# An attention stage whose steps all get new positions, and the row-sum reciprocals of the stage behind it set closer together

## The chip, the cores and the metric

The kernel runs on one core of a Trainium2 chip. The metric is device time in microseconds (us), the median of several executions. TensorE is called PE below, VectorE DVE, ScalarE ACT, GpSimd POOL, and SyncE, which here only issues transfers, SP. Each engine runs its own instructions strictly in the order in which they stand in the program.

## The reference

```python
q_pool = q.reshape(B, H, S // 2, 2, D).mean(axis=3)          # B, H, S, D = 8, 8, 1152, 64
scores = np.matmul(q_pool, k.transpose(0, 1, 3, 2)) / np.sqrt(D)
scores = scores - np.max(scores, axis=-1, keepdims=True)
attn = np.exp(scores)
attn = attn / (np.sum(attn, axis=-1, keepdims=True) + 1e-09)
x = merge_heads(np.matmul(attn, v))                          # [8, 576, 512]
theta = x @ w_theta
y = einsum('ts,bsd->btd', w_tok_r, x * cos(theta)) + einsum('ts,bsd->btd', w_tok_i, x * sin(theta))
u = x + y
out = u + np.maximum(u @ w_ch, 0.0)
```

Everything is float32. The kernel keeps that precision by splitting an operand into a rounded high part and the remainder (hi and lo), and adding up three products.

## The kernel before

**Part 1, attention.** The work is cut into 32 pairs of heads, numbered i. A pair passes through these steps, named as in the table `PLACE`:

- SP: `load_q`, `load_k`, `load_v`; `load_max` brings the transposed row maxima (tile nt, L818) back as rows nmrs (L829, L833).
- DVE: `pool_q` (L713) adds neighbouring rows of Q. POOL: `diff` (L720) prepares K. DVE turns the tiles: `t1` (L747, 960 columns) and `t0` (L745, 768 columns), into a PSUM bank each. ACT rounds them, `hi1`, `hi0` (L774), DVE takes the remainders, `lo1`, `lo0` (L778).
- PE and DVE: 15 passes for the row maxima. `pm` (L791) makes one block of scores from the high parts alone, `mx` (L803) reduces it. After `mx22`, the last, come `nm` (L815) and `nt` (L818).
- PE, ACT, POOL: 18 blocks of exact scores, `e` (L851), whose exponentials are taken by `x` (L861, tile pc) with the maxima that ACT's `rn` (L836, tile nmrr) has rounded. POOL adds them up, `ss` (L868). PE multiplies with V, `av` (L873), and sums over partitions, `ns` (L894).
- The reciprocals of the sums: `norm_recip` (L920). For the first eight pairs they are multiplied in here (`norm_out`, L944; `norm_turn`, L949), for the others in part 2.

The maxima of pair i+2 run beside the scores of pair i+1 and the products with V of pair i, so one period of this pipeline is one pair. Beside it, 18 small jobs prepare the weights (`w_max` L1027, `w_shift` L1031, `w_sign` L1038, `w_mask` L1044 on DVE; `w_mul`, `w_add` on POOL; ten `w_turn` on PE). They are "side" steps.

The order is made on the host before the program is built. `operations` lists every step with its engine, and `schedule` sorts each engine's steps by `PLACE[step] + 18 * i`, for the weights by `w0 + wd * job + wk * step`; it decides when side steps are put in, and it may look a few steps ahead at the start and the end. A score tile of PSUM is a bank: `t`, `pm`, `e`, `av` and `ns` share four pairs of them, and a step that takes a bank waits until its last reader is done. So a `pm` that takes over the bank of `t1` waits for `lo1`.

**Part 2, token and channel mixing.** Eight batches b follow each other, each step put at a number `at2(...)` (56 to a batch). For b > 1, the reciprocals for each quarter c of x are loaded by `dnload` (L1190) into the tile dn, of which there is one, and multiplied in by `dnmul` (L1194); then `xblock` (L1218, L1219) stores x turned, POOL makes the remainder xl (L605), and PE computes the angles pth (L1237). PE works on batch b-1 meanwhile: py (L1325), pr (L1364), the step `relu` (L1377), which DVE does and which frees PE's bank, and the output stores (`oblock`, L1385 and L1388). `dnload` and `dnmul` stand at:

```python
at2(base + DN_AT[0] + 0.1 + DN_AT[1] * c, dnload, b, c)
at2(base + DN_AT[0] + DN_AT[2] + DN_AT[1] * c, dnmul, b, c)
```

Of the kernel before, what the change touches and what calls it, by code (L numbers as in the profile page):

```python
# [22 lines left out]
NU = 18  # L23
CHAINS = ((0, 0, 0), (0, 1, 0), (0, 0, 1), (0, 1, 1), (0, 0, 2), (0, 1, 2), (0, 2, 0), (1, 0, 0), (0, 2, 1), (1, 0, 1), (0, 2, 2), (1, 0, 2), (1, 1, 0), (1, 2, 0), (1, 1, 1), (1, 2, 1), (1, 1, 2), (1, 2, 2))
PLACE = {
# [40 lines left out]
}  # L66
LOOK = 8
LATE = 2.0
# [11 lines left out]
THETA_AT = (-42.4, -33.8, -25.1, -15.4, -9.2)  # L80
XHI0_AT = 568.5
XB_AT = -55.0
DN_AT = (-79.5, 6.8, 6.4)
TH0_BANK = "hmmrh"
XN_AT = -4.0
XN0_BANK = "tmmrt"
# [422 lines left out]
def pooled_attention_moe_kernel(  # L509
# [638 lines left out]
    with ExitStack() as p2:  # L1148
# [17 lines left out]
        def at2(pos, fn, *args):  # L1166
            todo2.append((pos, len(todo2), fn, args))
# [251 lines left out]
        for b in range(B):  # L1419
            base = CYC * b  # L1420
            if b > 0:
                at2(base + DN_AT[0] if b > 1 else X1_AT, xload, b)
                if b > 1 and b % 2 == 0:
                    at2(base + DN_AT[0] + 0.2, dwload, b)
                    at2(base + DN_AT[0] + DN_AT[2] + 0.1, dwmul, b)
                for c in range(ND if b > 1 else 0):
                    at2(base + DN_AT[0] + 0.1 + DN_AT[1] * c, dnload, b, c)
                    at2(base + DN_AT[0] + DN_AT[2] + DN_AT[1] * c, dnmul, b, c)
            if b == 0:
# [75 lines left out]
```

## Time and profile before

| | us |
|---|---|
| median of 3 runs | 1281.33 (1281.25 to 1281.88) |
| profiled execution | 1282.72 |
| span in its trace | 1280.9 |
| PE busy | 1223.0 (95%) |
| DVE busy | 959.9 (75%) |
| POOL busy | 809.3 (63%) |
| ACT busy | 676.9 (53%) |

The numbers below are from the profiled execution, which is 1.39 us above the median; 1.8 us of it lie outside the span. The granted clock is 0.998 of full speed. Part 1 takes about 800 us of the span. The average busy share says little here: PE is nearly always busy, so a step's place matters only where PE stops for it.

### The profile page before, as it was taken

What the parts mean: (1) busy time and instruction counts of PE and PEld (TensorE: products, weight loads), DVE (VectorE), ACT (ScalarE), POOL (GpSimd) and SP (SyncE); (2) the same over time, 40 slices, a digit from 0 to 9 for tenths busy, and PEclk for the clock granted to TensorE, in tenths of its full rate; (3) what the DMA queues carried; (4) which work ended last, traced back from release to release, by engine and by line L of the source; (5) the groups of instructions that cost most, each with busy time, mean ns of one, the idle gap of its engine ahead of it and who ended that gap; (6) DMA issues with size and microseconds to landing.
All of it is one profiled execution on the core that took longest, in us unless ns stands there. A gap on an engine that the chain in (4) does not pass through costs nothing.

```text
span 1280.9 us, 27779 instructions
## 1 busy us (share of the span) xinstructions
PE 1223.0 (95%) x10915; PEld 952.1 (74%) x10915; DVE 959.9 (75%) x1313; ACT 676.9 (53%) x1129; POOL 809.3 (63%) x596
## 2 busy tenths in 40 slices
PE   4899999999999999999999999999999999999998
PEld 2566666666766666666666666698999999989998
DVE  6788898998788888878887887255675757657553
ACT  1456656656666665666565666464343443344331
POOL 1588988898887898788888788533423233242320
PEclk9999999999999999999999999999999999999999
DMA  7435555557455454545545541216654646455332
GB/s 119 83 77 134 110 96 123 127 115 158 85 101 93 104 120 85 113 92 100 117 90 104 90 98 39 62 57 150 127 102 105 134 109 135 95 120 116 85 55 37
DMA packets 489403, 130.16 MB, mean 102 GB/s; under 512 B 459576, under 2 KB 460280, under 8 KB 489272
## 3 DMA queue, kind: packets, MB, share of 16 engines
q1 hardware_dynamic: 489272, 128.39, 48.8%
q8 instruction: 85, 1.39, 0.5%
q14 instruction: 46, 0.38, 0.1%
HBM read 97.61 MB, written 29.52 MB: 99 GB/s over the span
## 4 chain that ended last, share of the span: by engine, by line
PE 67%; DVE 11%; ACT 8%; DMA 5%; issue 3%; SPq 3%; POOL 3%; ACTq 0%; DVEq 0%; POOLq 0%
PE b L851 17%; PE b L873 16%; PE py L1325 12%; PE b L791 6%; PE pr L1364 6%; PE pth L1237 5%; ACT pc L861 5%; PE b L894 4%; DVE mx L803 3%; DMA dn<-rod 2%; DMA qn<-in_q_dram 1%; POOL xl L605 1%; POOL ss L868 1%; DMA qk<-in_k_dram 1%; DVE wf L1038 1%
## 5 line engine op out<-in xcount | busy, mean ns | idle before, releaser
L803 DVE TENSOR_REDUCE mx<-b 128x2 f32<-128x768 f32 x480 | 440.4, 951 | 94.8 <-PE b L791 93.7
L868 POOL TENSOR_TENSOR ss<-ss,pc 128x576 f32<-128x576 f32 x314 | 460.9, 1480 | 14.4 <-ACT pc L861 2.0
L861 ACT ACTIVATE pc<-b 128x576 f32<-128x576 f32 x576 | 353.7, 652 | 128.8 <-PE b L851 112.7
L873 PE MATMUL b<-pc,vn 128*64 128x288 f32 x2304 | 306.8, 411 | 0.0
L873 PEld LDWEIGHTS b<-pc,vn 128*64 128x64 f32 x2304 | 154.4, 136 | 111.5 <-issue 21.8
L1325 PE MATMUL py<-wtk,Z 128*128 128x288 f32 x1728 | 234.2, 296 | 0.5 <-DVE uT L1377 0.5
L1325 PEld LDWEIGHTS py<-wtk,Z 128*128 128x128 f32 x1728 | 232.3, 189 | 2.0 <-DVE uT L1377 0.9
L1298 POOL TENSOR_TENSOR Z<-ab,Z 128x512 fp32r<-128x512 f32 x40 | 53.8, 1346 | 266.2 <-ACT Z L1294 266.2
L791 PE MATMUL b<-hi 64*128 64x384 f32 x960 | 180.0, 393 | 24.0 <-DVE mx L803 16.6
L851 PE MATMUL b<-hi 64*128 64x288 f32 x1152 | 191.4, 328 | 11.1 <-ACT pc L861 3.4
L851 PE MATMUL b<-lo,hi 64*128 64x288 f32 x1152 | 171.3, 293 | 0.0
L851 PE MATMUL b<-hi,lo 64*128 64x288 f32 x1152 | 170.8, 292 | 0.0
L791 PEld LDWEIGHTS b<-hi 64*128 64x128 f32 x960 | 90.2, 189 | 93.8 <-DVE mx L803 45.4
L851 PEld LDWEIGHTS b<-hi 64*128 64x128 f32 x1152 | 108.8, 185 | 52.6 <-ACT pc L861 41.4
L868 POOL TENSOR_TENSOR ss<-pc,pc 128x576 f32<-128x576 f32 x64 | 92.1, 1440 | 71.8 <-ACT pc L861 71.7
L851 PEld LDWEIGHTS b<-lo,hi 64*128 64x128 f32 x1152 | 109.8, 187 | 0.0
L851 PEld LDWEIGHTS b<-hi,lo 64*128 64x128 f32 x1152 | 109.5, 186 | 0.0
L1364 PEld LDWEIGHTS pr<-us,wch 128*128 128x128 f32 x768 | 104.1, 188 | 1.5
L1364 PE MATMUL pr<-us,wch 128*128 128x288 f32 x768 | 105.1, 295 | 0.0
L720 POOL TENSOR_TENSOR qk<-qk 128x384 f32<-128x384 f32 x62 | 64.4, 1038 | 64.2 <-DMA qk<-in_k_dram 54.2
L774 ACT CAST hi<-b 128x960 fp32r<-128x960 f32 x64 | 56.3, 881 | 63.2 <-DVE b L747 58.3
L778 DVE TENSOR_TENSOR lo<-b,hi 128x960 fp32r<-128x960 f32 x64 | 66.6, 1053 | 15.1 <-ACT hi L774 13.2
(100 smaller groups left out, 1326.1 us busy)
## 6 DMA issues: line engine op xcount, KB each, us to landing
vn<-in_v_dram SPq DMA_DIRECT2D x32, 576.0 KB
qn<-in_q_dram SPq DMA_DIRECT2D x124, 144.0 KB
qk<-in_k_dram SPq DMA_DIRECT2D x124, 144.0 KB
xd<-xu SPq DMA_DIRECT2D x32, 288.0 KB
xT<-xd SPq DMA_DIRECT2D x8, 1152.0 KB
xn<-xbd SPq DMA_DIRECT2D x140, 64.0 KB
out_dram<-ub SPq DMA_DIRECT2D x124, 72.0 KB
xbd<-xb SPq DMA_DIRECT2D x28, 288.0 KB
```

Of the source, the lines that this page charges most:

```text
L720: (nc.vector if op.eng == DVE else nc.gpsimd).tensor_tensor(kn[:, c : c + W], kn[:, c : c + W], kn[:, c - W : c], ALU.subtract)
L774: nc.scalar.copy(hi, src)
L778: nc.vector.tensor_tensor(lo, src, hi.bitcast(F32), ALU.subtract)
L791: nc.tensor.matmul(pm[:, h, 0:W], hi[hs, q : q + P], hi[hs, group(g)], start=(g == 0), stop=True, skip_group_check=(g > 0),)
L803: nc.vector.tensor_reduce(maxima(op.i)[:, at, g : g + 1], slots[op.slot][:, :, 0:W], AX.X, ALU.max)
L851: nc.tensor.matmul(pe[:, h, 0:HALF], w[hs], x[hs], start=bool(op.acq and n == 0), stop=(n == len(terms) - 1), skip_group_check=not op.acq,)
L861: nc.scalar.activation(pc, slots[op.slot][:, :, 0:HALF], AF.Exp, scale=SC)
L868: nc.gpsimd.tensor_tensor(st["ss", u], first, st["pc"][u, k], ALU.add)
L873: nc.tensor.matmul(half(op)[hs, 0:HALF], st["vn"][:, h, key(u, k), :], st["pc"][u, k][:, h, :], start=(k == 0), stop=(k == KT - 1),)
L1237: nc.tensor.matmul(th, xs[c][:, j * P : (j + 1) * P], ws[:, c], start=(n == 0), stop=(n == 11))
L1325: nc.tensor.matmul(st["py", c, u][:, 0:HALF], Z[zi][:, c * P : (c + 1) * P], wtk[wi][:, kw, u * HALF : (u + 1) * HALF], start=(i == 0 and ...
L1364: nc.tensor.matmul(pr[u][:, 0:HALF], wch[wi][:, c, e * P : (e + 1) * P], st["us", ui][:, c, u * HALF : (u + 1) * HALF], start=(n == 0), st ...
```

## The change

All numbers in `PLACE` are new, so the steps of part 1 stand in another order on every engine, and two of the three numbers of `DN_AT` are smaller. No step is added or taken away, and no other line differs. Of the table two lines stand for all:

```diff
-    "hi10": -21.08587, "lo10": -23.99859, "t00": -24.04688, "hi00": -19.4519, "lo00": -23.47768,
+    "hi10": -21.37568, "lo10": -31.19797, "t00": -30.74071, "hi00": -21.12643, "lo00": -29.5554,
...
-    "ns50": -3.42739, "slack": 0.08481, "turn": 18.16883, "w0": 1.55551, "wd": 33.42062,
-    "wk": 1.74585, "lk": 1, "early00": 8.02425, "xhi00": 525.23001, "xlo00": 492.64828,
+    "ns50": 213.87592, "slack": 0.14937, "turn": 0.45204, "w0": 16.49569, "wd": 33.25011,
+    "wk": 0.28685, "lk": 1, "early00": -61.74543, "xhi00": 523.75714, "xlo00": 622.34897,
...
-DN_AT = (-79.5, 6.8, 6.4)
+DN_AT = (-79.5, 6.2, 6.0)
```

**Place A, DVE in part 1, between nt and the first maxima of the next pair.** Before, in pair 12, which carries a weight job (b1 and b2, b0 and b3 are banks; hi12 and lo12 belong to pair 12):

```order
L818 STREAM_TRANSPOSE nt_135<-nm_133 128x32
L747 STREAM_TRANSPOSE b3_110<-qk12_3446 128x2x480
L745 STREAM_TRANSPOSE b0_107<-qk12_3446 128x2x384
L778 TENSOR_TENSOR lo12_3749<-b3_110,hi12_3748 128x960
L778 TENSOR_TENSOR lo12_3749<-b0_107,hi12_3748 128x768
L803 TENSOR_REDUCE mx12_3782<-b3_110 128x2
L1027 TENSOR_SCALAR ws_3787<-wf_3714 128x576
L1031 TENSOR_SCALAR wf_3714<-ws_3787 128x3x192
L803 TENSOR_REDUCE mx12_3782<-b0_107 128x2
L1038 SCALAR_TENSOR_TENSOR wf_3714<-raw_3552,wf_3714 128x3x192
L803 TENSOR_REDUCE mx12_3782<-b3_110 128x2
```

And of the changed kernel, the same place:

```order
L818 STREAM_TRANSPOSE nt_135<-nm_133 128x32
L747 STREAM_TRANSPOSE b1_108<-qk12_3451 128x2x480
L1027 TENSOR_SCALAR ws_3748<-wf_3701 128x576
L778 TENSOR_TENSOR lo12_3751<-b1_108,hi12_3750 128x960
L745 STREAM_TRANSPOSE b2_109<-qk12_3451 128x2x384
L1031 TENSOR_SCALAR wf_3701<-ws_3748 128x3x192
L778 TENSOR_TENSOR lo12_3751<-b2_109,hi12_3750 128x768
L1038 SCALAR_TENSOR_TENSOR wf_3701<-raw_3545,wf_3701 128x3x192
L803 TENSOR_REDUCE mx12_3804<-b1_108 128x2
L803 TENSOR_REDUCE mx12_3804<-b2_109 128x2
L803 TENSOR_REDUCE mx12_3804<-b1_108 128x2
```

The turn `t0` now stands behind `lo1`, so t and lo alternate, and the weight steps moved from between the first maxima to between t and lo. In pairs without a weight job the three rows are absent in both. Further along in each period, `pool_q` now stands ahead of `mx20` (before: behind it), and `norm_recip` between `mx21` and `mx22` (before: behind `mx42`). On PE, `pm40` and `pm30` used to come after ten of the sixteen `av` that follow `pm22`, with one `e` between them; now 13 `av` and all of `e16`, `e17`, `e18` come ahead of them, and the two stand together. The number of changes between `pm`, `e` and `av` in a period is the same.

**Place B, ACT at the end of pair 0's scores** (hi2 is the high part of pair 2, whose bank the first maxima of that pair need; pc0_16 is an exponential). Before:

```order
L861 ACTIVATE pc0_17_489<-b2_109 128x576
L774 CAST hi2_520<-b3_110 128x960
L836 CAST nmrr_128<-nmrs_126 128x576
L885 COPY xu0_535<-b1_108 128x288
L861 ACTIVATE pc0_16_543<-b0_107 128x576
L774 CAST hi2_520<-b2_109 128x768
L861 ACTIVATE pc0_18_560<-b0_107 128x576
```

Changed:

```order
L861 ACTIVATE pc0_16_494<-b3_110 128x576
L861 ACTIVATE pc0_17_499<-b2_109 128x576
L774 CAST hi2_512<-b1_108 128x960
L774 CAST hi2_512<-b2_109 128x768
L861 ACTIVATE pc0_18_554<-b3_110 128x576
L836 CAST nmrr_128<-nmrs_126 128x576
L885 COPY xu0_572<-b0_107 128x288
```

The second cast no longer stands behind the rounding of the maxima, a copy and `x16`, but right behind the first.

**Place C, SP in part 2, while batch 5 is begun and batch 6 is loaded** (dn6_2 are the reciprocals of batch 6, quarter 2; ub4 the output of batch 4). Before:

```order
L1227 DMA xn5_4_13567<-xbd5_93 32x16x32 x4
L1388 DMA out_0_dram<-ub4_1_13605 192x3x32 x4
L1388 DMA out_0_dram<-ub4_2_13616 192x3x32 x4
L1190 DMA dn6_2_13622<-rod6_102 64x576 x2
L1388 DMA out_0_dram<-ub4_3_13668 192x3x32 x4
L1190 DMA dn6_3_13679<-rod6_102 64x576 x2
```

Changed:

```order
L1227 DMA xn5_4_13567<-xbd5_93 32x16x32 x4
L1388 DMA out_0_dram<-ub4_1_13605 192x3x32 x4
L1190 DMA dn6_2_13614<-rod6_102 64x576 x2
L1388 DMA out_0_dram<-ub4_2_13619 192x3x32 x4
L1190 DMA dn6_3_13667<-rod6_102 64x576 x2
L1388 DMA out_0_dram<-ub4_3_13672 192x3x32 x4
```

Two loads pass four output stores each; the other batches from 2 on are alike. On DVE, in the same stretch, the multiplication of quarter 1 (L1194) now stands ahead of L1265 and L1266 of the angles and so two rows earlier before the `relu` of e = 2, and that of quarter 2 ahead of the `relu` of e = 3 instead of behind it. PE, ACT and POOL keep their order in part 2.

## Rows read from the trace of the kernel before

**Rows 1.** Busy us (instructions) by stretch: PE, PEld, DVE, ACT, POOL; clock; DMA share, GB/s.

```profile
38.40:96.80 58.40, 52.97 (x502) 37.13 (x502) 47.85 (x56) 32.37 (x54) 44.65 (x34) 1.00 0.45 87
96.80:798.60 701.80, 683.39 (x7075) 469.27 (x7073) 600.31 (x745) 440.63 (x741) 601.41 (x436) 1.00 0.51 104
```

**Rows 2.** Timeline of DVE, the operation nt alone: start, duration, engine, line, operation.

```profile
109.00 0.21 DVE L818 STREAM_TRANSPOSE nt<-nm 128x32 f32<-128x32 f32 x1
...
304.60 0.21 DVE L818 STREAM_TRANSPOSE nt<-nm 128x32 f32<-128x32 f32 x1
...
329.95 0.21 DVE L818 STREAM_TRANSPOSE nt<-nm 128x32 f32<-128x32 f32 x1
...
354.00 0.21 DVE L818 STREAM_TRANSPOSE nt<-nm 128x32 f32<-128x32 f32 x1
...
772.81 0.21 DVE L818 STREAM_TRANSPOSE nt<-nm 128x32 f32<-128x32 f32 x1
```

**Rows 3.** Timeline of all engines, 312 to 316 us; idle time before, and releaser, in brackets.

```profile
312.35 2.00 DVE L1038 SCALAR_TENSOR_TENSOR wf<-raw,wf 128x576 uint32<-128x576 uint32 x1
...
312.58 0.61 PE L791 MATMUL b<-hi 64*128 64x384 f32 x4 [0.25 <-DVE mx L803]
...
315.27 0.45 PE L791 MATMUL b<-hi 64*128 64x384 f32 x2 [0.91 <-DVE mx L803]
```

**Rows 4.** Timeline of all engines in a pair without weight job, 378 to 384 us.

```profile
378.33 5.07 PE L873 MATMUL b<-pc,vn 128*64 128x288 f32 x40
...
379.58 1.19 DVE L747 STREAM_TRANSPOSE b<-qk 128x960 f32<-128x960 f32 x1
380.68 0.95 DVE L745 STREAM_TRANSPOSE b<-qk 128x768 f32<-128x768 f32 x1
...
380.81 0.96 ACT L774 CAST hi<-b 128x960 fp32r<-128x960 f32 x1 [2.22 <-DVE b L747]
...
381.80 2.20 DVE L778 TENSOR_TENSOR lo<-b,hi 128x960 fp32r<-128x960 f32 x2 [0.17 <-ACT hi L774]
...
382.21 0.80 ACT L774 CAST hi<-b 128x768 fp32r<-128x768 f32 x1
...
383.33 0.44 PE L791 MATMUL b<-hi 64*128 64x384 f32 x2
```

**Rows 5.** Timeline of all engines around the second `lo` of pair 2.

```profile
63.73 0.96 DVE L778 TENSOR_TENSOR lo<-b,hi 128x768 fp32r<-128x768 f32 x1 [4.33 <-ACT hi L774]
...
64.75 0.44 PE L791 MATMUL b<-hi 64*128 64x384 f32 x2 [1.02 <-DVE lo L778]
```

**Rows 6.** Timeline of all engines around `pool_q`, 373 to 378 us.

```profile
374.19 1.43 POOL L868 TENSOR_TENSOR ss<-pc,pc 128x576 f32<-128x576 f32 x1 [0.18 <-ACT pc L861]
...
374.66 0.96 DVE L803 TENSOR_REDUCE mx<-b 128x2 f32<-128x768 f32 x1 [0.83 <-PE b L791]
...
375.53 0.75 DVE L713 TENSOR_TENSOR qk<-qn 128x576 f32<-128x576 f32 x1
375.58 1.97 POOL L868 TENSOR_TENSOR ss<-ss,pc 128x576 f32<-128x576 f32 x1
```

**Rows 7.** All instances of L713: duration ns minimum, median, maximum.

```profile
L713 DVE TENSOR_TENSOR qk<-qn x31: 746/748/1891, 27.7 to 767.2; 128x576 f32<-128x576 f32 x31
```

**Rows 8.** Timelines of SP, DVE and PE in part 2, batch 6 being loaded.

```profile
1122.03 5.70 SPq L1388 DMA_DIRECT2D out_dram<-ub  x8
...
1122.78 0.76 DVE L1194 TENSOR_TENSOR xT<-xT,dn 128x576 f32<-128x576 f32 x1 [1.18 <-DMA dn<-rod]
...
1132.46 0.76 DVE L1194 TENSOR_TENSOR xT<-xT,dn 128x576 f32<-128x576 f32 x1 [4.66 <-DMA dn<-rod]
...
1123.96 14.61 PE L1325 MATMUL py<-wtk,Z 128*128 128x288 f32 x106 [0.52 <-DVE uT L1377]
...
1143.02 0.50 PE L1237 MATMUL pth<-wth,xl 128*128 128x512 f32 x1 [1.51 <-POOL xl L605]
```

**Rows 9.** Timeline of PE in part 2, the same place while batch 4 is loaded.

```profile
1032.05 0.50 PE L1237 MATMUL pth<-wth,xl 128*128 128x512 f32 x1 [0.93 <-POOL xl L605]
```

74 rows, old and new, of the table PLACE are left out of this document.

## The prediction

> **What bounds the kernel now.** I read the page first: its share of busy time and its chain of waits both name PE. Since the change adds no work, it can only give or take time in which PE stands still, so the second view is busy time by stretch [rows 1]. The reader should subtract: of 1280.9 - 1223.0 = 57.9 us of idle PE in the span, 701.8 - 683.4 = 18.4 us lie in the 29 periods of the steady attention, and 58.4 - 53.0 = 5.4 us in the stretch from 38.4 us, about where the exact scores begin, to there [rows 1]. Most of the rest is loading and the first maxima, one after the other, and the last outputs.
>
> Third, the length of single periods, from one `nt` to the next [rows 2]: 25.35 us, then 24.05. The short one is a pair without a weight job; the 27 periods from 109.00 to 772.81 have a mean of 24.59 [rows 2], and the short ones, about half, agree within 0.07. The long ones carry a weight job, most of them a `w_turn`, about 0.9 us of PE's own work, which stays. The rest, here 1.2 us, is waiting: `pm` stands for 0.25 and 0.91 us because `w_sign` holds DVE for 2.00 us between two maxima [rows 3].
>
> **Term 1, the start.** In the period in which pair 0's scores are made, `lo0` of pair 2 leaves DVE idle for 4.33 us, since its `hi0` on ACT (0.80 us by [rows 4]) stands behind the row maxima, a copy and an exponential; PE then waits 1.02 us [rows 5]. Place B takes that away: the two casts follow each other, so `hi0` comes some 4 us earlier and `lo0` with it. Moved past it are one rounding, one copy and one exponential on ACT, under 2 us in all, and they are late by 0.8 us at most, the length of the cast. In steady pairs PE idles 18.4 / 701.8 x 58.4 = 1.5 us in a stretch of this length, here 5.4, so 3.9 us is the most that a perfect order from 38.4 us on would return. I take 3.0, bounds -1 and -5 (the lower one includes that the first maxima before 38.4 us also come a little sooner).
>
> **Term 2, a period without weights.** Place A makes DVE wait. From [rows 4]: `t1` runs from 379.58 to 380.77, `hi1` from 380.81 to 381.77, `lo1` from 381.80. Now `t0` starts only behind `lo1` (half of 2.20, more exactly 1.16), at about 382.9, and ends at 383.85; `hi0` takes 0.80 and `lo0` starts at 384.7 and ends at 385.7, where it used to end at 384.0. So DVE idles about 1.0 us twice, and `lo0` is 1.7 us late. What hides this is PE: `pm40` used to come after ten `av`, which take 5.07 us [rows 4], 0.5 each. Three more `av` (1.5 us) and two more `e` (0.4 each) now come ahead of it, so it is wanted 2.3 us later, at 385.6 instead of 383.33 [rows 4]. `pm40` takes over the bank of `t1`, free at 383.0, and `pm30` that of `t0`, wanted at 385.9 and free at 385.7. So the delay is covered, with 0.2 to 0.6 us to spare. Were the cover gone, it would be 1.7 us a pair. The other moves of a period (reciprocal, copies) fill idle time. I take -0.07 us a pair, since `pm30` and `pm40` now share one change of operand and no `e` stands between them; bounds -0.2 and +0.1; over 28 pairs -2.0 (-5.6 to +2.8).
>
> **Term 3, the weight jobs.** They are put into the two new DVE gaps: `w_max` and `w_shift`, about 0.75 us, fit into 1.0. That removes waits like those of [rows 3]. They sum up to about 5 us: 27 periods exceed 24.05 by 663.8 - 649.4 = 14.4 [rows 2], of which some ten `w_turn` take 9. But `w_sign` now stands behind `lo0` in seven pairs, with up to 2.00 us [rows 3] and no spare time left there; at some 0.7 to 0.8 us for each of them, that is about 5 us given back. I take -0.5 (-5 to +4), the 0.5 for `w_turn` that now stand among `av`.
>
> **Term 4, part 2.** Eight output stores hold SP for 5.70 us, to 1127.7; only then is dn of quarter 2 loaded, and its multiplication comes at 1132.46, after 4.66 us of idle DVE [rows 8]. Place C lets it pass four stores, 2.85 us. The single dn tile is free by then: quarter 1 is multiplied at 1122.78 and done at 1123.54. Quarter 3 passes four more, and then waits for quarter 2 as before. So xl comes 2.8 us earlier, and the wait of 1.51 us before pth [rows 8] goes, as does the 0.93 of batch 4 [rows 9]. Against it, in batch 6: the multiplication of quarter 1 waits 1.18 us for its transfer [rows 8], and L1265 and L1266 (1.1 us together) now stand behind it, ahead of the `relu` for which PE's py already waits 0.52 us [rows 8]. That wait grows by 1.1. `relu` of e = 3 becomes some 4 us late, but only a bank that is wanted much later hangs on it. Sum -1.5 - 0.9 + 1.1 = -1.3; bounds -2.5 and 0.
>
> **Sum.** -3.0 - 2.0 - 0.5 - 1.3 = -6.8 us, against the profiled 1282.7 as against the median of 1281.3, 1.4 lower: 1275.9 for a profiled execution, 1274.5 for the median.
>
> **A rule weighed.** `pool_q` has a median of 0.75 us, but a maximum of 1.89 [rows 7]; and the `ss` that starts 0.05 us after it takes 1.97 instead of 1.43 us [rows 6]. The Trainium skill (SBUF — State Buffer, "SBUF: two separate sides") says that a VectorE operation with two SBUF inputs and a GpSimd operation exclude each other for a whole instruction, and whichever starts first wins. The rows agree, with 1.97 against 1.43 and 1.89 against 0.75. What follows from them here is the second rival.
>
> **Rivals.**
> *No change that counts.* The weight steps' waits come back elsewhere in full, so term 3 is +3, and the period is 24.05 as before, so term 2 is 0. The sum is -3.0 + 0 + 3 - 1.3 = -1.3, which gives 1280, and 1278.7 to 1282 with a little more or less of the start. For it: every gap that DVE has in the new order is as long as what is put there, and PE is 97% busy in the steady stretch anyway. Against it: term 1 and term 4 don't depend on it.
>
> *Slower, by `pool_q`.* It used to stand behind `mx20`, now ahead of it. `mx20` starts at 374.66 after 0.83 us of idle time [rows 6], so DVE is free at 373.83 and `pool_q` can start some 0.3 us before `ss` does at 374.19 [rows 6]. If `ss` starts first, `pool_q` waits until 375.62 and ends at 376.4, `mx20` is 1.7 us late, and `pm21`, which writes the same bank, with it; about 1 us of that stays on PE, since `mx20` itself waits 0.83 us for PE so far. It decides when more than 7 of 28 pairs lose: then the gain is gone. Half of them give 1274.5 + 14 = 1288, all 1302. For it: a margin of 0.3 us, with x on ACT earlier in some pairs. Against it: where both orders keep PE and ACT alike up to here, the margin is the same in each pair.
>
> *A larger gain.* The start gives 5, the jobs' waits go for good (-5), and the period falls by 0.2 us since PE changes operands at better places: -5 - 5 - 1.3 and up to -5 more, 1265 to 1270. For it: that much idle time is there [rows 1]. Against it: seven `w_sign` in a place without reserve.
>
> **How the numbers follow.** The forecast's case 0.50, a larger gain 0.19, no change 0.18, slower by `pool_q` or by a cover of term 2 that is too thin 0.13. What can be told from no change is 0.2%, 2.6 us. The forecast's own bounds reach from 1269 to 1280; a tenth of it, and nearly all of the second case, lie within 0.2%. Range 1266 to 1284, which leaves out the lower end of the larger gain and most of the slower case. Faster 0.67, same 0.19, slower 0.14.
>
> **What the changed profile would show.** From `nt` to `nt` about 24.0 us without a job and 24.9 with one (term 2, 3); DVE idle about 1 us ahead of each `lo`, filled where a weight job runs; no wait of PE for `lo` near 64 us, and the first `nt` of a steady pair some 3 us earlier (term 1); no wait for xl in batches 4 and 6 and one of about 1.6 us for `relu` in batch 6 (term 4). I am wrong if `pool_q` shows a mean far above 0.8 us, if `pm30` waits for `lo` in every period, or if PE's idle time in the steady stretch is 18 us again.

## The result, and the profile after

The changed kernel takes 1267.38 us (median of 4 runs, 1266.41 to 1270.58), the kernel before 1281.45 beside it: 0.9894 of the time, 95% interval 0.9877 to 0.9912. That is 14.1 us less, where 6.8 less was forecast; the profiled execution took 1267.24 us with a span of 1265.5. The page, its head, busy times and chain:

```profile
span 1265.5 us, 27679 instructions
...
PE 1219.0 (96%) x10915; PEld 945.9 (75%) x10915; DVE 957.6 (76%) x1313; ACT 678.7 (54%) x1129; POOL 800.5 (63%) x596
...
PE 73%; ACT 8%; DVE 8%; POOL 4%; issue 3%; DMA 3%; SPq 1%; ACTq 0%; DVEq 0%; POOLq 0%
```

The span is 15.4 us shorter, PE's busy time only 4.0: most of the gain is idle time of PE. Where it lay is read from busy time by stretch (us, then PE, PEld, DVE, ACT, POOL; clock). The first two answer to [rows 1]; the third is as long as the first period of the exact scores and begins 0.28 us ahead of it (PE's first pass of L851 is at 38.12 us, that of pair 1 at 63.14):

```profile
38.40:96.80 58.40, 57.05 (x566) 39.21 (x566) 51.13 (x60) 35.82 (x59) 48.84 (x37) 1.00 0.54 101
96.80:798.60 701.80, 690.00 (x7145) 470.71 (x7141) 597.42 (x746) 446.04 (x747) 600.15 (x442) 1.00 0.51 103
37.84:62.87 25.03, 24.14 (x220) 16.92 (x220) 21.20 (x25) 13.47 (x21) 18.03 (x14) 1.00 0.39 61
```

Idle PE falls from 5.43 to 1.35 us in the start's stretch and from 18.41 to 11.80 in the long one (which in the changed kernel reaches some 13 us further into the work). The same period in the kernel before (first passes at 38.41 and 66.99 us):

```profile
38.40:66.97 28.57, 25.09 (x216) 18.03 (x216) 21.07 (x25) 14.19 (x22) 21.15 (x16) 1.00 0.48 84
```

It lost 3.5 us: 2.6 of idle time (3.48 to 0.89) and 0.95 of PE's own busy time. Next, `nt` on DVE, of pairs 3, 16, 17, 18, 26, 27, 30 and 31 (answers to [rows 2]):

```profile
103.72 0.21 DVE L818 STREAM_TRANSPOSE nt<-nm 128x32 f32<-128x32 f32 x1
...
421.33 0.21 DVE L818 STREAM_TRANSPOSE nt<-nm 128x32 f32<-128x32 f32 x1
...
445.19 0.21 DVE L818 STREAM_TRANSPOSE nt<-nm 128x32 f32<-128x32 f32 x1
...
468.97 0.21 DVE L818 STREAM_TRANSPOSE nt<-nm 128x32 f32<-128x32 f32 x1
...
662.80 0.21 DVE L818 STREAM_TRANSPOSE nt<-nm 128x32 f32<-128x32 f32 x1
686.55 0.21 DVE L818 STREAM_TRANSPOSE nt<-nm 128x32 f32<-128x32 f32 x1
...
761.38 0.21 DVE L818 STREAM_TRANSPOSE nt<-nm 128x32 f32<-128x32 f32 x1
785.45 0.21 DVE L818 STREAM_TRANSPOSE nt<-nm 128x32 f32<-128x32 f32 x1
```

and pairs 26, 27 and 31 of the kernel before:

```profile
675.17 0.21 DVE L818 STREAM_TRANSPOSE nt<-nm 128x32 f32<-128x32 f32 x1
699.23 0.21 DVE L818 STREAM_TRANSPOSE nt<-nm 128x32 f32<-128x32 f32 x1
...
798.21 0.21 DVE L818 STREAM_TRANSPOSE nt<-nm 128x32 f32<-128x32 f32 x1
```

Three numbers follow. Pair 3 comes 5.3 us sooner (109.00 [rows 2] to 103.72): the start. From there to pair 31, 28 periods take 681.7 instead of 689.2 us: 7.5 for the steady part. The remaining 2.6 of the span lie behind the `nt` of pair 31, nearly all of them in part 2. And a pair without a weight job (pair 26) takes 23.75 instead of 24.06 us; pair 16, with all four DVE steps of a job, 23.86.

Around such a pair, timeline of all engines in the kernel before (`lo0`, then `pm30`; `x00`, then `e02`):

```profile
383.04 0.96 DVE L778 TENSOR_TENSOR lo<-b,hi 128x768 fp32r<-128x768 f32 x1
...
384.06 0.44 PE L791 MATMUL b<-hi 64*128 64x384 f32 x2
...
388.26 0.65 ACT L861 ACTIVATE pc<-b 128x576 f32<-128x576 f32 x1 [0.74 <-PE b L851]
...
389.00 0.37 PE L851 MATMUL b<-hi 64*128 64x288 f32 x2
```

and after, pair 17 (`pm40` and `pm30` are one row of x4):

```profile
450.47 0.96 DVE L778 TENSOR_TENSOR lo<-b,hi 128x768 fp32r<-128x768 f32 x1 [0.86 <-ACT hi L774]
...
451.58 0.51 PE L791 MATMUL b<-hi 64*128 64x384 f32 x4
...
454.15 0.65 ACT L861 ACTIVATE pc<-b 128x576 f32<-128x576 f32 x1 [0.49 <-PE b L851]
...
455.14 0.30 PE L851 MATMUL b<-hi 64*128 64x288 f32 x2
```

Before, `pm30` starts 0.06 us behind the end of `lo0` (384.00), whose bank it takes, and `e02` 0.09 behind `x00` (388.91). PE follows DVE and ACT on their heels, yet no bracket shows it: the shortest waits that any row lists are of about 0.15 us. After, `lo0` ends at 451.43; `pm40` starts 0.15 later and `pm30`, the second half of its row, about 0.33 later; `e02` comes 0.34 us behind `x00`. Here neither of the two waits.

### The profile page after: what moved, and what is told of

Its sections match the earlier page's. It is cut to its first block, busy times and chain, and to the rows that moved or that the text cites. A ratio compares the mean times of both kernels' runs of the same rounds, so it can differ in the third digit from the quotient of the medians.

```text
span 1265.5 us, 27679 instructions
## 1 busy us (share of the span) xinstructions
PE 1219.0 (96%) x10915; PEld 945.9 (75%) x10915; DVE 957.6 (76%) x1313; ACT 678.7 (54%) x1129; POOL 800.5 (63%) x596
## 4 chain that ended last, share of the span: by engine, by line
PE 73%; ACT 8%; DVE 8%; POOL 4%; issue 3%; DMA 3%; SPq 1%; ACTq 0%; DVEq 0%; POOLq 0%
PE b L873 19%; PE b L851 17%; PE py L1325 14%; PE b L791 6%; PE pr L1364 6%; PE pth L1237 6%; ACT pc L861 5%; PE b L894 4%; POOL ss L868 2%; DVE mx L803 2%; DMA dn<-rod 1%; DVE lo L778 1%; ACT hi L774 1%; DVE kk L1261 1%; DVE b L745 1%
## 5 line engine op out<-in xcount | busy, mean ns | idle before, releaser
L868 POOL TENSOR_TENSOR ss<-ss,pc 128x576 f32<-128x576 f32 x314 | 447.8, 1447 | 7.9 <-ACT pc L861 0.3
L861 ACT ACTIVATE pc<-b 128x576 f32<-128x576 f32 x576 | 348.8, 652 | 159.7 <-PE b L851 141.2
L791 PE MATMUL b<-hi 64*128 64x384 f32 x960 | 179.1, 389 | 20.2 <-DVE mx L803 14.1
L851 PE MATMUL b<-hi 64*128 64x288 f32 x1152 | 189.6, 325 | 7.3 <-ACT pc L861 1.1
L868 POOL TENSOR_TENSOR ss<-pc,pc 128x576 f32<-128x576 f32 x64 | 96.6, 1509 | 122.5 <-ACT pc L861 122.4
L851 PE MATMUL b<-lo,hi 64*128 64x288 f32 x1152 | 170.6, 292 | 0.0
L851 PE MATMUL b<-hi,lo 64*128 64x288 f32 x1152 | 170.3, 292 | 0.0
L851 PEld LDWEIGHTS b<-hi 64*128 64x128 f32 x1152 | 108.5, 185 | 49.2 <-ACT pc L861 26.3
L851 PEld LDWEIGHTS b<-lo,hi 64*128 64x128 f32 x1152 | 109.1, 186 | 0.0
L851 PEld LDWEIGHTS b<-hi,lo 64*128 64x128 f32 x1152 | 108.9, 185 | 0.0
L778 DVE TENSOR_TENSOR lo<-b,hi 128x960 fp32r<-128x960 f32 x64 | 67.5, 1056 | 39.7 <-ACT hi L774 39.6
L1237 PE MATMUL pth<-wth,xh 128*128 128x512 f32 x288 | 72.7, 394 | 2.3 <-DVE r L1263 2.3
```

Of the source, the lines that this page charges most:

```text
L778: nc.vector.tensor_tensor(lo, src, hi.bitcast(F32), ALU.subtract)
L791: nc.tensor.matmul(pm[:, h, 0:W], hi[hs, q : q + P], hi[hs, group(g)], start=(g == 0), stop=True, skip_group_check=(g > 0),)
L851: nc.tensor.matmul(pe[:, h, 0:HALF], w[hs], x[hs], start=bool(op.acq and n == 0), stop=(n == len(terms) - 1), skip_group_check=not op.acq,)
L861: nc.scalar.activation(pc, slots[op.slot][:, :, 0:HALF], AF.Exp, scale=SC)
L868: nc.gpsimd.tensor_tensor(st["ss", u], first, st["pc"][u, k], ALU.add)
L1237: nc.tensor.matmul(th, xs[c][:, j * P : (j + 1) * P], ws[:, c], start=(n == 0), stop=(n == 11))
```

## The experiments

Intervals are of the ratio to the kernel before, run beside each group; the shared median of before was 1282.71, 1282.42 and 1281.86 us. Line numbers of kernels with added lines are higher than those above by these lines.

**Part 2 alone** (dn_only): the kernel before with

```diff
-DN_AT = (-79.5, 6.8, 6.4)
+DN_AT = (-79.5, 6.2, 6.0)
```

> The kernel before with the two new numbers of DN_AT alone; all of part 1 is as before. Theory (term 4 of the prediction): the waits for xl of 0.93 us (batch 4) and 1.51 + 0.16 us (batch 6) go, and the wait for relu in batch 6 grows from 0.52 by up to 1.1 us, so the time falls by 1.3 us, 0 to 2.5. Rival: part 2 gains the 2.7 us by which the changed kernel's profile is ahead of the profile before from the first pxn to the end; then it falls by 2.7.

1280.95 us, 0.9988 (0.9980 to 0.9997): 1.5 us faster. Both waits for xl are gone from its trace. `relu` is waited for 0.95 us, and a wait of 1.24 us for L1341 ahead of another py, at 923.5 us, is new:

```profile
1125.49 14.63 PE L1325 MATMUL py<-wtk,Z 128*128 128x288 f32 x106 [0.95 <-DVE uT L1377]
```

**The start of the table alone** (start_only): the kernel before, with the new positions for pairs 0 and 1 only.

```diff
-        op.pos = PLACE[op.place] + op.off
+        op.pos = (OTHER if 0 <= op.i <= 1 else PLACE)[op.place] + op.off
```

> The kernel before, with the positions of pairs 0 and 1 alone taken from the new table. Theory A (the start pays because PE, once it begins the scores of pair 0, runs without a break and so leaves the stretch of slow matmuls about 4.5 us earlier): the first e of pair 1 comes about 2.5 us or more earlier than before, and the time falls by 2.5 to 4.5 us, although the second cast of pair 2 still stands behind x16. Theory B (the start pays through the cast of pair 2, place B): nothing changes up to pair 1, and the time falls by less than 1 us.

1302.01 us, 1.0154 (1.0136 to 1.0172). It decides nothing on the start: the two tables don't fit together at the seam, where PE waits 2.51 and 2.75 us, and by its trace the granted clock is at half for 24 us in all between 63.5 and 138.7 us.

**Another number for changes of operand** (turn_border): the changed kernel with

```diff
-"turn": 0.45204
+"turn": 18.16883
```

> The changed kernel with one number of its table as before (turn: 18.16883 for 0.45204): the planner then puts eight of the ten w_turn between av16 and e18, where PE changes its kind of work anyway, instead of into the middle of av or between e and pm. Theory (a w_turn costs 1.3 to 2.0 us where it now stands, against 0.9 before, by an extra change of work and by the wait for the bank that it holds): periods with a w_turn fall from about 25.5 to 24.8, and the time by 4 to 6 us, to about 1262. Rival (the cost is the work itself, or the wait for the bank wherever it stands): within 2 us of the changed kernel.

1282.80 us, 1.0003 (0.9994 to 1.0012). The number also orders the start anew: the first scores of pairs 0 and 1 stand at 38.65 and 72.77 us, 34.1 apart instead of 25.0, and the granted clock is at half for 6.8 us of that, from 64.2 us on. So the whole time does not test the place of `w_turn`; the single periods do. Most pairs without a `w_turn` still take 23.72 to 23.91; pairs 8, 9, 11 and 25 take 24.1 to 26.9, with waits of 0.34 to 1.88 us. Those with a `w_turn` take 25.4 to 25.7, in the changed kernel 25.1 to 25.8, so a place between the products and `e18` is no cheaper.

**`e18` between `pm40` and `pm30`** (split_e18): the changed kernel with

```diff
-"e18": 19.27409
+"e18": 19.56
```

> The changed kernel with e18 put back between pm40 and pm30 (one number of the table). Theory (half of the 0.25 us that a period without a weight job lost comes from pm40 and pm30 standing together): such periods go from 23.80 to about 23.93, and the time rises by 3 to 4 us, to about 1271. Rival A (all of the 0.25 us hangs on it): +7 us. Rival B (the period is set elsewhere): no change.

1273.50 us, 0.9927 (0.9913 to 0.9941), some 4 us above the changed kernel by the two ratios. But pairs 17 and 28, without weight jobs, take 23.75 and 23.72 us, in the changed kernel 23.78 and 23.72. That the two `pm` stand together is therefore not why the period is shorter. In the periods the loss is in six pairs (24.3 to 24.6 us) and pair 25 (25.9), in which the planner has put weight steps elsewhere, and in pair 30 (24.4).

**One product ahead of `pm40`** (av_ahead): the kernel before, and behind the planner

```diff
...
+    for op in order:
+        if (op.name, op.a, op.b) == ("av", 1, 4) and 4 <= op.i <= 27:
+            n = next(k for k, o in enumerate(out) if (o.name, o.i, o.a, o.b) == ("pm", op.i + 2, 4, 0))
+            out.insert(n, op)
...
```

> The kernel before, in which one product of the attention, av 1|4 of pair i, stands ahead of pm40 of pair i+2 instead of behind pm30 (24 pairs, i from 4 to 27). Nothing else moves. In the trace of before, pm30 starts 0.05 us behind the end of lo0 in most pairs (it takes over the bank that lo0 reads), and the step behind it takes 0.37 us instead of 0.27; in the kernel after, pm30 starts 0.33 us behind lo0. Theory (the shorter period without a weight job comes in part from this wait, too short to be shown as idle time): with 0.49 us more of av ahead, pm30 stands 0.3 us or more behind lo0, and a period without a weight job falls by about 0.14 us, to 23.9 to 24.0; 24 x 0.14 = 3.4, so the time is 2 to 4 us below that of before. Rival (the shorter period comes from the order of the operands alone, not from lo0): the period stays at 24.04 to 24.11 and the time is that of before within 1 us.

**The same and `e00` ahead of `pm31`** (two_moves): besides, `pm31` of pairs 6 to 29 is held back until `e00` has been put out.

> The kernel before with two moves on PE in 24 pairs and nothing else: av 1|4 of pair i ahead of pm40 of pair i+2 (as in av_ahead), and e00 of pair i ahead of pm31 of pair i+1 instead of behind pm31 and pm41. In the trace of before e02 starts 0.09 to 0.10 us behind the end of x00, in that of after 0.34 us behind it, since x00 there is made 0.24 us sooner. Theory (a period without a weight job is short by the sum of small waits that are not shown as idle time: 0.12 for lo0, as av_ahead gave, and 0.06 for x00): such a period takes 23.86 to 23.95 us, 0.06 below av_ahead's. Rival (only lo0's wait counts): 23.92 to 23.99 as in av_ahead. The time itself is within 3 us of before, since the periods with a weight job got longer in av_ahead.

1283.07 us, 1.0007 (0.9996 to 1.0017), and 1282.25, 1.0001 (0.9992 to 1.0009). Pair 26 in av_ahead:

```profile
677.04 0.21 DVE L829 STREAM_TRANSPOSE nt<-nm 128x32 f32<-128x32 f32 x1
700.97 0.21 DVE L829 STREAM_TRANSPOSE nt<-nm 128x32 f32<-128x32 f32 x1
```

and pairs 26 and 27 in two_moves:

```profile
673.90 0.21 DVE L835 STREAM_TRANSPOSE nt<-nm 128x32 f32<-128x32 f32 x1
697.79 0.21 DVE L835 STREAM_TRANSPOSE nt<-nm 128x32 f32<-128x32 f32 x1
721.65 0.21 DVE L835 STREAM_TRANSPOSE nt<-nm 128x32 f32<-128x32 f32 x1
```

The mean of pairs 17, 24 and 26, all without waits that are listed, is 24.07 in before, 23.94 with one move, 23.87 with both and 23.77 in the changed kernel. In av_ahead `pm30` of these pairs comes 0.49 us behind `lo0` instead of 0.06. So 0.13 us hung on `lo0` and 0.07 on `x00`, and 0.10 came from other moves. For the whole time I had expected 2 to 4 us from av_ahead. They did not show, because periods beside weight jobs got longer: pairs 5, 7 and 9, 24.99, 25.02 and 24.26 us in before, now take 25.97, 25.93 and 25.57, with waits of 0.97, 0.91 and 1.63 us.

**Less cover** (cover_less): the changed kernel, where the products 0|6, 0|7 and 1|6 are held back until `pm30` of two pairs on has been put out.

```diff
+MOVED = ((0, 6), (0, 7), (1, 6))
...
+        if op.name == "av" and 4 <= op.i <= 27 and (op.a, op.b) in MOVED:
+            held.setdefault(op.i, []).append(op)
+            continue
+        out.append(op)
+        if (op.name, op.a, op.b) == ("pm", 3, 0):
+            out.extend(held.pop(op.i - 2, []))
```

> The kernel after, in which three products of the attention, av 0|6, 0|7 and 1|6 of pair i, stand behind pm30 of pair i+2 instead of ahead of pm40 (24 pairs); t and lo still alternate on DVE, so lo0 is as late as in after, and pm30 is wanted 1.46 us sooner. Theory (the later lo0 is covered by the av ahead of pm40): pm30's reserve of 0.33 us is used up and PE waits about 1.1 us for lo in each of the 24 pairs; period 24.9 without a weight job, time 22 to 30 us above after, 1290 to 1297. Rival (lo0's place makes no difference, the av would have hidden nothing): time as after within 3 us, 1267 to 1270.

1297.51 us, 1.0125 (1.0109 to 1.0141), 30 us above the changed kernel by the ratios. Each period has the wait, and a pair without a weight job takes 25.0 (483.65 - 458.61); 24 times 1.25 is the 30:

```profile
464.89 0.44 PE L805 MATMUL b<-hi 64*128 64x384 f32 x2 [1.02 <-DVE lo L792]
```

**Weight steps not between t and lo** (w_not_in_gaps): the changed kernel with another list of candidates in the planner (the rest of its line is left out)

```diff
-main[e][: ahead(e)] + side[e][:1]
+main[e][: ahead(e)] + [o for o in side[e][:1] if not (main[e] and main[e][0].name in ("t", "lo") and o.name in ("w_max", "w_shift", "w_sign", "w_mask"))]
```

> The kernel after, in which the four DVE steps of a weight job (w_max, w_shift, w_sign, w_mask) may not be put between t1, lo1, t0 and lo0; the planner puts them in the next place behind lo0. Everything else is planned by the same table. Theory (the steps are free only in the gaps between t and lo; elsewhere they make PE wait between two maxima, as in before): waits of 0.2 to 0.9 us come back in some ten pairs, time 3 to 8 us above after, 1270 to 1275. Rival (the places don't matter, the steady gain is all in the period without a weight job): time as after within 1.5 us.

1278.87 us, 0.9976 (0.9966 to 0.9985): 10.5 us above the changed kernel by the ratios, more than the 3 to 8 expected. Waits of `pm` and `e` for maxima, `lo` or ACT stand in 15 of the 28 pairs (0.16 to 1.25 us each), in the changed kernel in four. The planner also puts the later steps elsewhere here; with this plan, most of the gain is lost.

**`w_turn` among the products** (turns_in_av): the changed kernel, with `w_turn` allowed only ahead of an `av` (the same line, cut).

```diff
+[o for o in side[e][:1] if not (o.name == "w_turn" and main[e] and 3 <= main[e][0].i <= 29 and not (main[e][0].name == "av"))]
```

> The kernel after, in which w_turn may stand only ahead of an av (pairs 3 to 29): five of them move from between exact scores or between av 0|7 and av 1|6 to av 0|1 | av 0|2, close to where they stood in before; the steps that follow are planned by the same table. In after a period with a w_turn is 1.3 to 2.0 us longer than one without, in before about 0.95. Theory (it is the place of w_turn that costs, since scores and maxima wait for its bank there): the five give back about 0.7 us each, time 2 to 5 us below after, 1262.5 to 1265.5. Rival (w_turn costs the same in any place, or what it frees comes back as a wait elsewhere): time as after within 1.5 us.

1271.03 us, 0.9912 (0.9897 to 0.9927): not faster than the changed kernel but 2.3 us above it by the ratios; the two intervals overlap. A wait of PE in a pair with a moved `w_turn`:

```profile
405.60 0.44 PE L791 MATMUL b<-hi 64*128 64x384 f32 x2 [0.94 <-ACT pc L861]
```

The waits for `wtk` behind `w_turn` are gone, but pairs 13, 15, 20 and 22 take 26.1 to 26.3 us, with waits for ACT and for maxima of 1.04 to 1.34 us together, and pair 25, without one, 26.25. The rival holds in substance: what one place frees comes back in another.

**Place B alone** (hi0_first): the kernel before, with `t0` and `hi0` of pair 2 written out ahead of the row maxima of pair 1.

```diff
...
+    held = [o for o in order if key(o) in (("t", 2, 0, 0), ("hi", 2, 0, 0))]
+    out = [o for o in order if o not in held]
+    n = next(k for k, o in enumerate(out) if key(o) == ("rn", 1, 0, 0))
+    return out[:n] + held + out[n:]
```

> The kernel before with one move: hi0 of pair 2 stands on ACT straight behind hi1 of pair 2, ahead of the row maxima, a copy and an exponential of pairs 0 and 1 (t0 of pair 2 is written out earlier too, but keeps its place on DVE). Theory (term 1 of the prediction): lo0 comes some 4 us earlier, PE's wait of 1.02 us for it goes, and the first e of pair 2 and all that follows come 1 us earlier: time 0.7 to 3 us below before. Rival (the gain at the start has nothing to do with this place): time as before within 0.5 us, and the wait is replaced by another of the same length.

1278.43 us, 0.9974 (0.9961 to 0.9987). PE's waits of 1.02 and 0.26 us are gone, and the period is 1.4 us shorter:

```profile
38.38:65.58 27.20, 24.74 (x218) 17.92 (x216) 21.11 (x25) 14.08 (x22) 20.20 (x16) 1.00 0.51 88
```

Of the median's 3.4 us, these 1.4 are shown. At the end of the attention 1.1 are left in the profile; the rest lies in part 2, whose steps are those of before. There the profile before has 3.41 us at half the granted clock (Term 4 below) and this one none; why the medians differ by as much, I can't say.

**PE's idle time ahead of the first scores filled** (early_rate, big_fill): the changed kernel, with matmuls that nobody reads ahead of `pm41` of pair 1; in early_rate 24 of them with 32 columns, in big_fill

```diff
+            if (op.i, j, g) == (1, 4, 1):
+                for n in range(14):
+                    hs = HEADS[n % 2]
+                    nc.tensor.matmul(
+                        slots[3][:, n % 2, 0:W], hi[hs, q : q + P], hi[hs, group(g)],
+                        start=True, stop=True, skip_group_check=True,
+                    )
```

> The kernel after, with 24 small matmuls more (64 x 128 by 32 columns, into columns that nothing reads) ahead of the first row maxima of pair 1, where PE stands idle for 4.78 us; they leave nothing out. In after, two passes of an exact score step follow each other by 0.24 to 0.25 us until 41.6 us and by 0.13 us from then on; in before the change comes at 46.4 us, and in both some 4 us after PE began to work without a break. Theory (part of the gain at the start is that PE gets to its full rate earlier, since it has work earlier): with the idle time filled, the passes follow each other by 0.13 us from about 38 us on, and the time is 1 to 3 us below after. Rival (the slow passes have another cause, such as the first use of a code or of a tile): the change of the rate stays at 41 to 42 us and the time is that of after within 0.7 us.

> The kernel after with 14 matmuls more of the size of those of the row maxima (64 x 128 by 384 columns, into a bank that is free there and read by nobody) in PE's idle time of 4.78 us ahead of 37.7 us; they leave nothing out. In early_rate 24 matmuls of 32 columns there did not bring the full rate sooner: the passes went from 0.24 to 0.13 us apart at 42.9 us, against 41.6 in after. Theory (the full rate follows some time behind the start of work without a break, if that work is of the usual size): the change comes at 36 to 39 us and the time is 1 to 3 us below after. Rival (the slow passes are bound to the first scores of the attention or to something else at that time): change at 41 to 43 us, time as after within 0.7 us.

1268.87 us, 0.9896 (0.9882 to 0.9909), and 1268.21, 0.9898 (0.9880 to 0.9916): both the time of the changed kernel, so the expected 1 to 3 us did not come in either. What they show of PE's rate stands in the last section. No version beats the changed kernel.

## Why the prediction was half right

The direction held, and so did the places that were named; the sum was half of what came. What happened is close to the rival of a larger gain (1265 to 1270, given 0.19), by its sizes for the start and the period, but not by its reasons. That the time lies inside the stated range, 1.4 us from its lower end, is in part luck: two of the terms came out beyond their own bounds.

**Term 1, the start: -3.0 forecast, -5.3 between the two profiles.** Place B does about what was said. After, timeline of `hi0`, `lo0` of pair 2 and the `pm` behind it (answers to [rows 5]):

```profile
59.52 0.80 ACT L774 CAST hi<-b 128x768 fp32r<-128x768 f32 x1 [2.12 <-DVE b L745]
60.35 0.96 DVE L778 TENSOR_TENSOR lo<-b,hi 128x768 fp32r<-128x768 f32 x1 [0.86 <-ACT hi L774]
...
60.96 0.85 PE L791 MATMUL b<-hi 64*128 64x384 f32 x4
```

`lo0` comes 3.4 us sooner and not 4, since between the casts ACT now waits 2.12 us for `t0`, which place A has put behind `lo1`. PE's wait for it fell from 1.02 to 0.06 us: the second `pm` of the third row starts at 61.37, `lo0` ends at 61.31. The mis-sized step is the one from this place to the whole stretch: hi0_first got 1.4 us from it. The bound (at most 3.9 us of idle time to gain from 38.4 us on) was about right, and it was reached: in the first two periods of scores idle time fell by 4.1. By the trace, PE's earlier waits of 0.45, 0.81, 0.18 and 0.63 us in the first of them went or shrank to 0.42, 0.20 and 0.17. Which moves took them away no run shows. I had counted only part of that bound, and neither the 0.3 us by which the first scores come sooner (38.41 to 38.12) nor PE's busy time, 0.95 us less in the first period and 0.46 more in the second.

Busy time is not all the order's. In two_moves, whose steps on PE, DVE and ACT stand as in before until 105 us, the first period is

```profile
38.31:64.30 25.99, 22.46 (x217) 15.64 (x216) 20.32 (x25) 13.75 (x22) 20.02 (x15) 1.00 0.53 93
```

It is 2.6 us shorter than before's, all of it busy time, with the same idle time (3.53 and 3.48 us), because PE came to its full rate sooner in that execution (last section). Its `nt` of pair 3 comes at 106.30 instead of 109.00 us. So the 5.3 us hold for these two executions; what the order shows is the idle time, 4.1 us less (3.4 against dn_only, whose idle time in these periods is 4.6).

**Term 2, the period: -0.07 a pair forecast, about -0.3 measured.** The core was right: t and lo alternate, `lo0` is late, and the products ahead of `pm40` cover it, with 0.2 to 0.6 us forecast and 0.33 found; cover_less shows the price of a thinner cover, 1.25 us a pair. The size was not: even the bound of -0.2 was passed. The failed step is the reason for the gain, "share one change of operand": split_e18 parts the two and keeps the period. What I had read past is in the kernel before: from [rows 4] and the rows next to it, `pm30` came 0.06 us behind `lo0`. In the order before, the cover was exactly used up; the longer one gave 0.13 us. Another 0.07 came from `e00`, which moved ahead of `pm31`, so that `x00` is ready for `e02`. Both are shown by av_ahead and two_moves; 0.10 stay unassigned. With 24.06 (pair 26 before) and 23.78 us (pair 17 after), over 28 pairs that is 7.8 us, slightly more than the steady part's 7.5.

**Term 3, the weight jobs: -0.5 forecast, about +0.4 measured, made up differently.** With the same 24.06 and 23.78 as bases, on which the split from term 2 hangs, eight periods with a `w_turn` (in before the period behind it, since it stands at a period's end) exceeded them by 10.0 us before and 13.4 after, the other twenty by 5.5 and 2.5. So the waits of [rows 3] went, 3 us; w_not_in_gaps gives more than that back when the steps leave the gaps. The forecast's 5 us for `w_sign` behind `lo0` did not come: of the seven pairs only pair 7 waits for a maximum there (0.91 us), and pair 16, with all four steps, takes 23.86. What came back instead was at `w_turn`, which I had credited with 0.5. Its timeline in pair 14:

```profile
377.20 0.66 PE L1093 MATMUL b<-ident,ws 128*128 128x128 f32 x4
378.00 0.86 ACT L1112 CAST wtk<-b 128x512 fp32r<-128x512 f32 x2 [1.01 <-PE b L1098]
378.89 1.00 DVE L1116 TENSOR_TENSOR wtk<-b,wtk 128x512 fp32r<-128x512 f32 x2 [0.91 <-ACT wtk L1112]
...
379.94 0.44 PE L791 MATMUL b<-hi 64*128 64x384 f32 x2 [0.57 <-DVE wtk L1116]
```

It takes a bank, ACT and DVE empty it within 2.7 us, and the next maxima wait 0.57 us for that. In five pairs PE waits 0.28 to 0.73 us for `wtk` behind a `w_turn`. In both experiments with other places for it, it cost no less.

**Term 4, part 2: -1.3 forecast, -1.5 measured** by dn_only, between its bounds. Timeline of PE after, the place of the fourth row of [rows 8], and DVE's multiplications in the same batch:

```profile
1110.89 14.63 PE L1325 MATMUL py<-wtk,Z 128*128 128x288 f32 x106 [0.98 <-DVE uT L1377]
```

```profile
1101.86 0.98 DVE L1194 TENSOR_TENSOR xT<-xT,dn 128x576 f32<-128x576 f32 x1 [1.06 <-DMA dn<-rod]
1108.65 0.76 DVE L1194 TENSOR_TENSOR xT<-xT,dn 128x576 f32<-128x576 f32 x1 [1.78 <-DMA dn<-rod]
1115.06 0.76 DVE L1194 TENSOR_TENSOR xT<-xT,dn 128x576 f32<-128x576 f32 x1 [1.35 <-DMA dn<-rod]
1120.36 1.75 DVE L1194 TENSOR_TENSOR xT<-xT,dn 128x576 f32<-128x576 f32 x1 [1.61 <-DMA dn<-rod]
```

The waits of 0.93 and 1.51 us for xl are gone; the multiplications come 5 to 7 us apart, where one waited 4.66 us [rows 8]. The wait for `relu` grew by 0.46 instead of 1.1, and one of 0.43 us was added at 910 us: net -1.55. From the `nt` of pair 31 to the end, the profile is 2.6 us shorter. Most of the rest fits a stretch of the kernel before, behind its wait of 2.14 us at 892.3, in which the granted clock is 0.50, the lower of TensorE's two levels of 1.2 and 2.4 GHz:

```profile
893.04:896.45 3.41, 3.41 (x9) 2.64 (x9) 2.94 (x7) 1.89 (x4) 0.00 (x0) 0.50 0.89 100
```

Half of these 3.41 us is an estimated 1.7 at most; av_ahead and two_moves, with the same part 2 and no such stretch, take 0.9 and 1.0 us less from that `nt` to the end. dn_only has such a stretch at 924.8 us, the changed kernel has none in part 2. It does not come from the order: PE is idle for 2.95 to 3.04 us in the 25 us up to that wait in all of these, and only in the profile before did the clock fall there.

**The rivals.** `pool_q` never lost its race: its durations in nanoseconds (minimum, median, maximum), where before one took 1891 [rows 7], are

```profile
L713 DVE TENSOR_TENSOR qk<-qn x31: 745/747/758, 26.9 to 756.0; 128x576 f32<-128x576 f32 x31
```

"No change that counts" fell with its two conditions: the period changed, and the start gave more than 3. Summed up: start -5.3, period -7.8, jobs +0.4 and part 2 -1.5 make -14.2, against -14.1 measured. That they agree so closely is chance, since the start alone differs by 2.7 us between two executions of one order.

## What to carry to other kernels

A row that starts within 0.1 us of the end of what it depends on can be a wait, even where the profile lists no idle time; two such places, 0.13 and 0.07 us in a period, are an estimated 5.6 us over 28 periods, though the whole time of two_moves did not show it. So before costing a longer cover at nothing, measure how much of the present one is left, from the end of the producer to the start of the consumer. And a stall that many small moves touch (here the start) is better sized by the idle time that can go at all than by the one wait that can be explained. And before a start is compared between two profiles, look whether the engine reached its full rate at the same time in both.

## What the runs showed of the hardware

PE began the first scores at half its later rate. The views print a granted clock of 1.00 for that time, but the trace's record of the granted clock begins only at 46.53 us in the kernel before and at 42.24 in the changed one, so nothing is recorded of what was granted ahead of that. What shows the rate is the distance of equal instructions: groups of two 288-column passes, whose two begin within 0.03 us of each other, follow by 0.24 us, 1.2 columns a nanosecond each, as at the lower of TensorE's levels of 1.2 and 2.4 GHz; later by 0.13. The change in the timeline of PE before:

```profile
45.94 0.44 PE L851 MATMUL b<-hi 64*128 64x288 f32 x2
46.18 0.44 PE L851 MATMUL b<-lo,hi 64*128 64x288 f32 x2
46.42 0.35 PE L851 MATMUL b<-hi,lo 64*128 64x288 f32 x2
46.60 0.30 PE L851 MATMUL b<-nmrr,oner 64*128 64x288 f32 x2
```

and in big_fill:

```profile
40.36 0.43 PE L858 MATMUL b<-hi 64*128 64x288 f32 x2
40.63 0.30 PE L858 MATMUL b<-lo,hi 64*128 64x288 f32 x2
40.76 0.30 PE L858 MATMUL b<-hi,lo 64*128 64x288 f32 x2
```

It came at 46.5 us before, at 42.2 in the changed kernel, 43.0 with the small fill and 40.5 with the large one, which is between the theory's 36 to 39 and the rival's 41 to 43. Before, PE had last stood idle (0.45 us) until 40.3, in the changed kernel (4.78 us) until 37.7, in big_fill (2.83 us) until 35.7; so it was not "some 4 us" in both, as early_rate's expectation has it. The Trainium skill (TensorE: Matmul & The Clock Gate, "Part 1: The HAM clock gate") says that TensorE starts at half its clock and gets the full one once it has been at work. That agrees with the half rate at the first scores in every run. What decides when it ends stays open. It is not the order alone: two_moves, with the order of before and the same wait of 0.45 us until 40.25, had the full rate from 39.7 us on, dn_only from 44.2, hi0_first from 46.2. So the fills, with one profile each, can't show that they moved it.

The worth in one execution is up to 2.6 us, the difference in busy time between before and two_moves above. In big_fill the first scores of pair 1 come 0.6 us sooner than in the changed kernel (62.53 for 63.14), and its median shows nothing that could be measured.
